# Banded attention and a two-layer product on one core: 200 transposes that nobody reads, two products moved behind the last first product, and a new order of every step

## The chip, the core and the metric

The kernel runs on one core of one Trainium2 chip. The metric is device time in microseconds (us). Three runs of the kernel before gave 1057.28, 1058.74 and 1061.05 us; the median is 1058.74.

## What is computed

The input has 8 batches of 8 heads, 512 local and 32 global positions each, 64 numbers per head. Local queries see local keys within 32 positions and all global keys; global queries see everything. The attention's output, 4352 rows of 512, then goes through a product with `w_in`, an exact GELU and a product with `w_out`. All is float32. Cut to what matters:

```
k_all, v_all = concat([k_g, k_l]), concat([v_g, v_l])
out_g = softmax(q_g @ k_all.T / 8) @ v_all
s_ll  = where(|i - j| <= 32, q_l @ k_l.T / 8, -1e9)
out_l = softmax(concat([q_l @ k_g.T / 8, s_ll])) @ v_all
x     = concat([out_g, out_l]) as rows of 512 (8 heads x 64)
y     = gelu(x @ w_in) @ w_out          # 512 -> 2048 -> 512
```

## The kernel before, in words

**Units and chunks.** The attention of one batch, one half (256 queries) and one pair of heads is a unit; there are 64, and they are numbered here u0, u1, ... in the order of the loop over `units`. Four units fill one chunk of 256 rows, which then goes through the two products. There are 16 such chunks, and a 17th, key `"g"`, of the 256 global rows.

**Steps of one unit.** `kp` and `qp` (L361 to L369): transposes on TensorE that turn keys and queries, copied out of PSUM to `kt` and `qt` (for the first eight units, `NPE`; later ones are transposed by VectorE, DVE). `s` (L439): scores. L458 on DVE adds the mask and takes the maximum; L322 on ScalarE (ACT) takes the exponentials into `a_t`; `sg` (L592) are the scores of the global queries. L488 to L492 on DVE scale by the sum, and L499 and L504, on DVE or GpSimd (POOL), make the edge pieces `ge`. `t` (L513 to L516): transposes of the probabilities, copied to `ao`. `o` (L562 for the first eight units, L549 later): probabilities times values, copied to `xs`.

**Steps of one chunk.** `xh` and `xl` split a row in a coarse part and a remainder, so that three fast products (L726 to L728) make up a float32 one. The first product, `h`, runs over 16 blocks f of 128 columns, each of four pieces over the input; `ml_g` takes the GELU of two blocks at once into `gf`, which is split in `gh` and `gl`; the second product (L757 to L759) adds two blocks' worth into the accumulators `acc0` and `acc1`. `ml_e` copies them to `ob`, and `ml_w` sends `ob` out.

**Weights.** `w_in` and `w_out` come in 32 pieces (`wl`, `wraw`); five steps (`w_1` to `w_5`: two on ACT, one shift on DVE, a cast and a subtraction) split each in two parts, kept in `wi` and `wo`. Of the first `WB` pieces, those with index 1, 2, 4 or 5 in each seven go through the pool `wb` (4 buffers), all others through `wa` (3 buffers). The space of `wb` is later used by `gf`, `gh`, `gl`, `xh` and `xl`.

**What sets the order.** Each step is a node with an engine or a choice of engines, a due time, needs, and buffers that it takes and frees. A list scheduler at the end of the function simulates the engines with the durations in `DUR` and, among the steps that can start first, takes the one due first; the due times are shifted per kind by the tables `OFF` (all) and `OFF0` (first chunk). Every engine then runs its steps in that order: an instruction that waits holds up all behind it on its engine.

PSUM is split in pools of two banks: `ps_s`, `ps_t`, `ps_h`, and `ps_o` with `acc0` and `acc1`. The first four blocks of the first chunk's `h` also use these two accumulators, so that the step `("hc", (0,0), 0, 0)` takes the buffer `acc`.

Of the kernel before, what the change touches and what calls it, by code (L numbers as in the profile page):

```python
# [8 lines left out]
F32 = mybir.dt.float32  # L9
# [4 lines left out]
AF = mybir.ActivationFunctionType  # L14
# [44 lines left out]

PORT = {"w3", "w4", "w5", "k2", "q1", "k1", "q2", "tgl", "b", "n", "nf", "ns", "vc", "vl", "gvc", "gvl", "xh", "xl", "gh", "gl", "gn"}  # L60

EARLY = {"gh": "a", "gl": "p", "gvc": "va", "gvl": "p", "k1": "a", "nf": "pv", "ns": "pv", "q1": "va", "vc": "va", "vl": "v", "xh": "va", "xl": "vp"}
LATER = {"gh": "va", "gl": "p", "gvc": "a", "gvl": "p", "k1": "va", "nf": "v", "ns": "pv", "q1": "va", "vc": "va", "vl": "p", "w4": "va", "w5": "pv", "xh": "a", "xl": "vp"}

OFF = {
    "ah": 3.7, "al": 7.1, "b": -0.8, "c": -23.8, "e": -38.8, "g": -16.9, "gagh": 2.4, "gagl": -24.7,
    "gah": -46.1, "gal": 17.6, "gex": 34.4, "gh": 11.4, "gl": 15.6, "glv": -3.1, "gmin": -0.7,
    "gn": 10.2, "go": -12.2, "gsh": 11.8, "gsl": -92.2, "gt": -6.0, "gvc": -51.6, "gvl": 28.8,
# [3 lines left out]
    "sga": -22.9, "sgc": -11.8, "t": 0.3, "tg": -5.3, "tgh": -13.8, "tgl": -30.7, "tk": 50.0,  # L72
    "tq": 106.4, "vc": -12.9, "vl": -42.1, "vm": -35.6, "w1": 67.7, "w2": -35.9, "w3": 0.2,
    "w4": 1.4, "w5": -5.6, "wl": 4.2, "x": 20.7, "xh": -24.9, "xl": -12.1,
}
OFF0 = {
    "ah": 6.2, "al": 2.7, "b": -8.0, "c": -4.3, "e": 8.2, "g": -11.9, "gagh": -12.8, "gagl": -27.4,
    "gah": 23.2, "gal": -25.7, "gex": 19.5, "gh": 2.9, "gl": 2.2, "glv": -5.1, "gmin": -5.1,
    "gn": -23.1, "go": 34.0, "gsh": -28.1, "gsl": -33.9, "gt": 7.9, "gvc": 55.3, "gvl": -10.2,
# [12 lines left out]
HQ = 4  # L92
NPE = 8
UNP = 100
WB = 14


@with_exitstack
def attn_mlp(ctx, tc, q_l, k_l, v_l, q_g, k_g, v_g, w_in, w_out, out):
    nc = tc.nc  # L100
    B, H, S, D = q_l.shape
    SG = q_g.shape[2]
    DM = H * D
# [10 lines left out]
    ap_ = ctx.enter_context(tc.tile_pool(name="ap", bufs=1))  # L114
# [557 lines left out]
    def gu_o(e, g, i):  # L672
        a = [late["agt"][:, n] for n in range(4)] + [late["agg"][:, i]]
        o = ps_s.tile([P, 2, 2, D], F32, name="go", tag="s")
        st[g, "o"] = o
        for n in range(5):
            nc.tensor.matmul(out=o, lhsT=a[n].rearrange("p h l q -> p (h l q)"),  # L677
                             rhs=late["vgs"][:, 2 * n:2 * n + 2], start=(n == 0), stop=(n == 4))

    def gu_sh(e, g, i):  # L680
        o = st[g, "o"]
        t = ap_.tile([P, 2, D], F32, name="gos", tag="gos")
        st[g, "os"] = t
        nc.scalar.activation(out=t, in_=o[:, :, 1, :], func=AF.Copy)

    def gu_sl(e, g, i):
        t = st[g, "os"]
        nc.vector.tensor_add(out=t, in0=st[g, "o"][:, :, 0, :], in1=t)

    def gu_x(e, g, i):  # L690
        t = ps_s.tile([P, 2, 2, SG], F32, name="gx", tag="s")
        st[g, "x"] = t
        nc.tensor.transpose(out=t, in_=st[g, "os"], identity=ident)

    def gu_yh(e, g, i):
        st[g, "c"] = c = ap_.tile([P, SG], F32, name="gc", tag="gc")
        for j in range(2):
            pr = slice(64 * j, 64 * j + 64)
            nc.scalar.activation(out=c[pr], in_=st[g, "x"][pr, j, 1, :], func=AF.Copy)

    def gu_yl(e, g, i):
        b, p = g[0], 2 * g[1] + i
        for j in range(2):
            pr = slice(64 * j, 64 * j + 64)
            nc.vector.tensor_add(out=late["xg"][pr, p, b * SG:b * SG + SG], in0=st[g, "x"][pr, j, 0, :], in1=st[g, "c"][pr])


    def ml_xh(e, key, p):
# [108 lines left out]
    for n, u in enumerate(units):  # L817
# [25 lines left out]
        else:  # L843
# [52 lines left out]
        if g and odd:  # L896
# [9 lines left out]
            for i in range(2):  # L906
# [11 lines left out]
                step(("gyh", g, i), gu_yh, (g, i), "a", g0 + 7.0 + 2 * i, [("gx", g, i)], [("gc", (g, i))])  # L918
                step(("gyl", g, i), gu_yl, (g, i), "v", g0 + 7.3 + 2 * i, [("gyh", g, i)], [], [("s", (g, i, "x")), ("gc", (g, i))])

    LAG = LAGS
    for n, key in enumerate(keys):
        C0, W = C * n, C / NF
# [209 lines left out]
```

## Time and profile before

| What | us |
|---|---|
| median of three runs | 1058.74 |
| the profiled execution's own time | 1058.35 |
| its span, first to last instruction | 1056.5 |
| TensorE busy | 1023.0 (97%) |
| ACT, DVE, POOL busy | 745.4, 716.1, 355.4 |

The profile is of one execution. PE is TensorE, SPq the queue from which SyncE issues DMAs. Lines are those of the kernel before. In a timeline a row gives the start, the duration from the first start to the last end of the instructions merged in it, engine, line, operation, output and inputs, and in brackets the idle time of the engine ahead of it with what ended it. Matmuls are pipelined: the time that one costs is the distance from its start to the next start, not its duration. In a table of stretches a row gives the stretch, its length, and for each engine the busy time with the number of instructions; then the granted clock of TensorE as a share of full speed, the DMA share and GB/s.

### The profile page before, as it was taken

To read this page: it belongs to the slowest core of one execution; us is meant where nothing else is said; L and a number is where in the kernel's file an instruction comes from. 1 tells how busy PE (TensorE), PEld (TensorE's weight loads), DVE (VectorE), ACT (ScalarE), POOL (GpSimd) and SP (SyncE) were. 2 spreads that over 40 slices of the span, in tenths; PEclk is the share of its full clock that TensorE was granted. 3 is DMA by queue.
4 is the path that set the end of the run, shared out by engine and by line. 5 is a ranking of instruction groups with operands and counts; after the bars stand their busy time and mean duration, and the time that the engine had idled before them with its cause. 6 is when DMAs were issued, how large, how long until landed. Compare 5 with 4: busy or idle time off the path is not lost.

```text
span 1056.5 us, 21637 instructions
## 1 busy us (share of the span) xinstructions
PE 1023.0 (97%) x7096; PEld 912.2 (86%) x7096; DVE 716.1 (68%) x2168; ACT 745.4 (71%) x1650; POOL 355.4 (34%) x407
## 2 busy tenths in 40 slices
PE   4799999999999999999999999999999999999997
PEld 3488789889899989998899988999899988999896
DVE  5898866775768767777868777677877778670000
ACT  5886887677769686787679677777778677873221
POOL 3232345334333434234323523233223433243120
PEclk9899999999999999999999999999999999999999
DMA  8656333322222332223222232223222332110000
GB/s 242 204 146 196 86 83 64 77 51 68 46 60 37 64 68 49 55 52 78 49 61 38 63 71 46 51 53 77 51 62 38 65 69 48 41 25 21 1 21 21
DMA packets 273233, 71.27 MB, mean 67 GB/s; under 512 B 258528, under 2 KB 266720, under 8 KB 273120
## 3 DMA queue, kind: packets, MB, share of 16 engines
q1 hardware_dynamic: 269808, 65.03, 27.5%
q10 hardware_dynamic: 3312, 4.85, 1.5%
q8 instruction: 56, 0.92, 0.4%
q14 instruction: 57, 0.47, 0.1%
HBM read 60.88 MB, written 8.91 MB: 66 GB/s over the span
## 4 chain that ended last, share of the span: by engine, by line
PE 88%; DMA 4%; ACT 3%; DVE 2%; SPq 1%; issue 1%; POOL 0%; ACTq 0%; DVEq 0%; POOLq 0%
PE h L726 12%; PE h L728 11%; PE h L727 11%; PE acc L757 11%; PE acc L758 11%; PE acc L759 11%; PE o L549 5%; PE s L439 5%; PE t L513 3%; PE go L677 2%; PE sg L592 2%; PE t L514 1%; DMA wraw<-in_moe_w_out_dram 1%; DMA wraw<-in_moe_w_in_dram 1%; ACT a_t L322 1%; DMA vr<-in_v_l_dram 1%
## 5 line engine op out<-in xcount | busy, mean ns | idle before, releaser
L163 POOL TENSOR_TENSOR gl<-gf,gh 128x512 fp32r<-128x512 f32 x135 | 177.2, 1312 | 461.7 <-DVE gh L158 259.9
L726 PE MATMUL h<-xh,wi 128*128 128x256 f32 x1088 | 314.9, 289 | 1.3 <-ACT xh L156 1.3
L727 PE MATMUL h<-xl,wi 128*128 128x256 f32 x1088 | 303.8, 279 | 0.7 <-POOL xl L163 0.4
L728 PE MATMUL h<-xh,wi 128*128 128x256 f32 x1088 | 303.6, 279 | 0.0
L757 PE MATMUL acc<-wo,gh 128*128 128x512 f32 x544 | 220.4, 405 | 1.4 <-ACT gh L156 1.4
L758 PE MATMUL acc<-wo,gl 128*128 128x512 f32 x544 | 215.5, 396 | 0.3 <-DVE gl L163 0.3
L759 PE MATMUL acc<-wo,gh 128*128 128x512 f32 x544 | 215.6, 396 | 0.0
L726 PEld LDWEIGHTS h<-xh,wi 128*128 128x128 f32 x1088 | 204.2, 188 | 12.5 <-ACT xh L156 1.7
L727 PEld LDWEIGHTS h<-xl,wi 128*128 128x128 f32 x1088 | 204.7, 188 | 7.2 <-DVE xl L163 0.6
L728 PEld LDWEIGHTS h<-xh,wi 128*128 128x128 f32 x1088 | 204.2, 188 | 0.0
L322 ACT ACT_TABLE_LOAD x129 | 165.5, 1283 | 40.3 <-PE h L728 38.6
L322 ACT ACTIVATE gf<-h 128x512 f32<-128x512 f32 x136 | 81.3, 598 | 78.8 <-PE h L728 76.2
L759 PEld LDWEIGHTS acc<-wo,gh 128*128 128x128 f32 x544 | 102.5, 188 | 24.6
L322 ACT ACTIVATE a_t<-a_t,sm 128x192 f32<-128x192 f32 (+1 forms) x256 | 117.0, 459 | 1.2 <-DVE sm L464 0.5
L757 PEld LDWEIGHTS acc<-wo,gh 128*128 128x128 f32 x544 | 102.5, 188 | 15.1 <-ACT gh L156 1.6
L758 PEld LDWEIGHTS acc<-wo,gl 128*128 128x128 f32 x544 | 102.7, 189 | 13.8 <-DVE gl L163 0.6
L163 POOL TENSOR_TENSOR vs<-vr,vs 128x512 fp32r<-128x512 f32 x56 | 72.7, 1298 | 120.0 <-ACT vs L156 56.3
L458 DVE CUSTOM_DVE_ANT_0 a_t<-s,mask 128x192 f32<-128x192 f32 (+1 forms) x256 | 80.8, 369 | 27.8 <-PE s L439 27.6
L533 DVE TENSOR_TENSOR at<-t,at 128x512 fp32r<-128x512 f32 x112 | 67.8, 619 | 23.6 <-ACT at L156 22.0
L156 ACT ACTIVATE at<-t 128x512 fp32r<-128x512 f32 x112 | 59.2, 542 | 23.9 <-PE t L516 10.4
L549 PE MATMUL o<-at,vs 128*128 128x256 f32 x448 | 74.3, 288 | 0.3 <-DVE sm L464 0.2
L549 PEld LDWEIGHTS o<-at,vs 128*128 128x128 f32 x448 | 63.0, 188 | 8.4 <-issue 2.1
(121 smaller groups left out, 1618.5 us busy)
## 6 DMA issues: line engine op xcount, KB each, us to landing
raws<-in_v_l_dram SPq DMA_DIRECT2D x64, 128.0 KB, 2.4
out_dram<-ob SPq DMA_DIRECT2D x32, 256.0 KB, 2.1
raws<-in_k_l_dram SPq DMA_DIRECT2D x224, 36.0 KB, 1.9
vr<-in_v_l_dram SPq DMA_DIRECT2D x116, 64.0 KB, 2.1
raws<-in_q_l_dram SPq DMA_DIRECT2D x224, 32.0 KB, 1.9
wraw<-in_moe_w_out_dram SPq DMA_DIRECT2D x12, 512.0 KB, 4.0
wraw<-in_moe_w_in_dram SPq DMA_DIRECT2D x11, 512.0 KB, 4.6
wraw<-in_moe_w_in_dram ACTq DMA_DIRECT2D x5, 512.0 KB, 4.4
```

Source lines behind the costliest of these rows:

```text
L156: nc.scalar.activation(out=out, in_=in_, func=AF.Copy)
L163: (nc.vector if e == "v" else nc.gpsimd).tensor_sub(**kw)
L322: nc.scalar.activation(func=func, **kw)
L458: nc.vector.tensor_tensor_reduce(out=a_t[:, j, aoff[half][i]:aoff[half][i] + w], in0=s[:, c:c + w], in1=masks[half][:, c:c + w], scale=1.0 ...
L533: nc.vector.tensor_sub(out=at[:, 1], in0=st.pop((u, "t", j))[:, :n * P].rearrange("p (n q) -> p n q", q=P), in1=at.bitcast(F32)[:, 0])
L549: nc.tensor.matmul(out=o[:, :, qsl], lhsT=l.rearrange("p s e -> p (s e)"), rhs=r, start=(n == 0), stop=(n == 3), skip_group_check=True)
L726: nc.tensor.matmul(out=h, lhsT=hi, rhs=xh, start=(c == 0 and not (key == (0, 0) and f < HQ and f % 2)), stop=False, skip_group_check=True)
L727: nc.tensor.matmul(out=h, lhsT=hi, rhs=xl, start=False, stop=False, skip_group_check=True)
L728: nc.tensor.matmul(out=h, lhsT=lo, rhs=xh, start=False, stop=(c == NCC - 1), skip_group_check=True)
L757: nc.tensor.matmul(out=acc[t], lhsT=gh[:, f % 2, tsl], rhs=hi, start=(f == 0), stop=False)
L758: nc.tensor.matmul(out=acc[t], lhsT=gl[:, f % 2, tsl], rhs=hi, start=False, stop=False)
L759: nc.tensor.matmul(out=acc[t], lhsT=gh[:, f % 2, tsl], rhs=lo, start=False, stop=(f == NF - 1))
```

## The change

A new step `dm` runs two 128x128 transposes of the identity into the bank `acc1`; nothing reads them. There are 100 such steps in a chain, due last of all, so that the scheduler puts one wherever TensorE would be idle by its own times. The first takes the buffer `acc` and the hundredth frees it, and the first chunk's first product takes the same buffer: it comes behind all 200 transposes. The first of them needs the first keys' transposes.

```
+    def st_dm(e, i):
+        if i == 0:
+            st["dm"] = ps_o.tile([P, DM], F32, name="dm", tag="acc1")
+        for n in range(2):
+            nc.tensor.transpose(out=st["dm"][:, n * P:n * P + P], in_=ident, identity=ident)
...
+NDM = 100
+NF32 = 8
...
+    for i in range(NDM):
+        step(("dm", i), st_dm, (i,), "t", 1e4, [("dm", i - 1) if i else ("tk", units[0])], [("acc", "dm")] if not i else [], [("acc", "dm")] if i == NDM - 1 else [])
```

In the chunk `"g"` the second products of blocks 12 to 15 now need the last piece of the last first product. Those of 14 and 15 needed it already, through the GELU; 12 and 13 are the two that move.

```
             step(("mo", key, f), ml_o, (key, f), "t", C0 + W * (f + LAG) + 1.0,
-                 [("gl", key, f // 2), ("mo", key, f - 1) if f else None, ("mo", keys[n - 1], NF - 1) if n and not f else None] + ([("w5", 2 * f + 1)] if not n else []),
+                 ([("hc", key, NF - 1, NCC - 1)] if key == "g" and f >= NF - 4 else []) + [("gl", key, f // 2), ("mo", key, f - 1) if f else None, ("mo", keys[n - 1], NF - 1) if n and not f else None] + ([("w5", 2 * f + 1)] if not n else []),
```

`WB` falls from 14 to 10, so that two weight pieces more go through the pool of three buffers. The planner's own durations and engines change in a few entries, and most of the shifts in `OFF` and `OFF0`; one line of many:

```
-    "tk": 0.65, "tkn": 0.75, "tqn": 0.45, "tq": 0.44, ...
+    "tk": 0.65, "tkn": 0.6, "tqn": 0.33, "dm": 0.22, "tq": 0.44, ...
...
-WB = 14
+WB = 10
...
-    "ah": 3.7, "al": 7.1, "b": -0.8, "c": -23.8, "e": -38.8, "g": -16.9, "gagh": 2.4, "gagl": -24.7,
+    "ah": 3.7, "al": 7.1, "b": -0.8, "c": -21.0, "dm": 16.9, "e": -33.2, "g": -16.9, "gagh": 8.1,
```

`NF32` names the units whose scores use unsplit keys and queries; it is 8 as `NPE` is, so nothing follows from it. The results of the global queries' step are kept per unit (`st[g, i, "o"]` for `st[g, "o"]`), so that two may be under way at once.

Because the due times move, the order of every engine is new. Three places follow. The first is TensorE around the start of the first product `h`. Before, it stands behind the scores of the sixth unit:

```order
L562 MATMUL o_597<-ao_593,vr 64x128
L562 MATMUL o_597<-ao_589,vr 64x128 x2
L439 MATMUL s<-kt,qt 128x192 x2
L439 MATMUL s<-kt,qt 128x224 x2
L369 MATMUL qp<-ident,raws 128x128 x2
L726 MATMUL h<-xh,wi 128x256
L727 MATMUL h<-xl,wi 128x256
L728 MATMUL h<-xh,wi 128x256
```

Ahead of it lie 7 `kp`, 7 `qp`, 6 `s`, 5 `sg`, 4 `t` and 4 `o`. In the changed kernel the same place reads:

```order
L572 MATMUL o_921<-ao_906,vr 64x128 x2
L332 MATMUL dm<-ident 128x128 x22
L602 MATMUL sg<-kt,gs 128x256
L332 MATMUL dm<-ident 128x128 x2
L523 MATMUL t<-ident,a_t_147 128x128 x2
L524 MATMUL t<-ident,ge 128x128
L526 MATMUL t<-ident,ge 128x128
L332 MATMUL dm<-ident 128x128 x2
L523 MATMUL t<-ident,a_t_147 128x128 x2
L524 MATMUL t<-ident,ge 128x128
L736 MATMUL h<-xh,wi 128x256
L737 MATMUL h<-xl,wi 128x256
```

Ahead of it now lie 8 `kp`, 8 `qp`, 7 `s`, 7 `sg`, 6 `t`, 5 `o` and the 200 transposes `dm`; the last `t` is that of u5. Behind it the first chunk's two products alternate without much between them.

The second place is ACT around the exponentials of the eighth unit, u7, which write `a_t_147`. Before, they follow the seventh GELU:

```order
L322 ACTIVATE gf<-h 128x512
L199 ACTIVATE wraw<-wraw 128x512
L203 ACTIVATE wraw<-wraw 128x512
L322 ACT_TABLE_LOAD
L322 ACTIVATE a_t_147,sm<-a_t_147,sm 128x192
L322 ACTIVATE a_t_147,sm<-a_t_147,sm 128x224
```

Now they follow the second:

```order
L324 ACTIVATE gf<-h 128x512
L205 ACTIVATE wraw<-wraw 128x512
L158 ACTIVATE gh<-gf 128x512
L188 DMA wraw<-in_moe_w_out_dram 128x1024
L201 ACTIVATE wraw<-wraw 128x512
L205 ACTIVATE wraw<-wraw 128x512
L324 ACT_TABLE_LOAD
L324 ACTIVATE a_t_147,sm<-a_t_147,sm 128x192
L324 ACTIVATE a_t_147,sm<-a_t_147,sm 128x224
```

Five GELUs and the weight steps between them have moved behind u7's exponentials.

The third place is the end of TensorE's program. The numbers of `gh` tell which blocks a second product uses. Before (`gh_13795` is of blocks 12 and 13, `gh_13837` of 14 and 15):

```order
L757 MATMUL acc0_13580<-wo_140,gh_13795 128x512
L758 MATMUL acc0_13580<-wo_140,gl_13797 128x512
L759 MATMUL acc0_13580<-wo_140,gh_13795 128x512
L757 MATMUL acc1_13581<-wo_140,gh_13795 128x512
L758 MATMUL acc1_13581<-wo_140,gl_13797 128x512
L759 MATMUL acc1_13581<-wo_140,gh_13795 128x512
L726 MATMUL h_13782<-xh_13479,wi_139 128x256
L727 MATMUL h_13782<-xl_13480,wi_139 128x256
L728 MATMUL h_13782<-xh_13479,wi_139 128x256
L757 MATMUL acc0_13580<-wo_140,gh_13837 128x512
L758 MATMUL acc0_13580<-wo_140,gl_13839 128x512
L759 MATMUL acc0_13580<-wo_140,gh_13837 128x512
```

And now (`gh_13996` is of blocks 12 and 13):

```order
L736 MATMUL h_13983<-xh_13680,wi_139 128x256
L737 MATMUL h_13983<-xl_13681,wi_139 128x256
L738 MATMUL h_13983<-xh_13680,wi_139 128x256
L767 MATMUL acc0_13781<-wo_140,gh_13996 128x512
L768 MATMUL acc0_13781<-wo_140,gl_13998 128x512
L769 MATMUL acc0_13781<-wo_140,gh_13996 128x512
L767 MATMUL acc1_13782<-wo_140,gh_13996 128x512
L768 MATMUL acc1_13782<-wo_140,gl_13998 128x512
L769 MATMUL acc1_13782<-wo_140,gh_13996 128x512
L767 MATMUL acc0_13781<-wo_140,gh_13996 128x512
L768 MATMUL acc0_13781<-wo_140,gl_13998 128x512
L769 MATMUL acc0_13781<-wo_140,gh_13996 128x512
```

Twelve matmuls, those of blocks 12 and 13, moved from between the last pieces of `h` to behind the last of them; the twelve of blocks 14 and 15 stay at the very end.

## Rows read from the trace of the kernel before

**Rows 1.** Busy time by stretch: stretch, length, busy per engine (instructions), clock, DMA.
```profile
56.70:200.00 143.30, 137.25 (x949) 121.20 (x949) 112.73 (x321) 111.73 (x246) 51.10 (x58) 0.99 0.46 113
189.00:200.00 11.00, 9.28 (x71) 8.46 (x70) 8.48 (x23) 8.07 (x18) 2.99 (x6) 1.00 0.42 94
200.00:1040.00 840.00, 839.92 (x5929) 758.73 (x5928) 561.44 (x1731) 588.52 (x1296) 288.26 (x312) 1.00 0.24 51
1045.00:1056.50 11.50, 5.05 (x15) 3.07 (x13) 0.69 (x1) 2.42 (x4) 0.00 (x0) 0.80 0.18 46
```
**Rows 2.** Timeline of TensorE, three stretches from 56 to 75: start, duration, instruction.
```profile
56.71 0.36 PE L726 MATMUL h<-xh,wi 128*128 128x256 f32 x1
...
64.36 0.38 PE L369 MATMUL qp<-ident,raws 128*128 128x128 f32 x2
64.58 0.38 PE L513 MATMUL t<-ident,a_t 128*128 128x128 f32 x2
...
65.44 0.97 PE L439 MATMUL s<-kt,qt 64*128 64x192 f32 x8
66.73 1.96 PE L562 MATMUL o<-ao,vr 128*64 128x128 f32 x16 [0.33 <-ACT ao L156]
...
74.36 0.59 PE L592 MATMUL sg<-kt,gs 128*128 128x256 f32 x2
74.60 0.58 PE L757 MATMUL acc<-wo,gh 128*128 128x512 f32 x1
```
**Rows 3.** Busy time by stretch, columns as in rows 1: up to the last `xl`.
```profile
15.30:58.30 43.00, 32.43 (x177) 23.65 (x177) 38.12 (x110) 37.62 (x96) 10.27 (x12) 0.88 0.72 210
```
**Rows 4.** Timeline of VectorE near 57 us.
```profile
56.70 1.63 DVE L163 TENSOR_TENSOR xl<-xs,xh 128x256 fp32r<-128x256 f32 x3
```
**Rows 5.** Timeline of GpSimd near 108 us: the edge pieces of one unit.
```profile
108.20 1.03 POOL L499 TENSOR_TENSOR ge<-a_t,sm 128x256 f32<-128x256 f32 x1 [9.52 <-DVE sm L489]
109.19 0.40 POOL L504 TENSOR_TENSOR ge<-a_t,sm 128x128 f32<-128x128 f32 x1
```
**Rows 6.** Timeline of TensorE, 20 to 25 us.
```profile
20.76 2.00 PE L439 MATMUL s<-kt,qt 64*128 64x192 f32 x8
22.69 0.69 PE L513 MATMUL t<-ident,a_t 128*128 128x128 f32 x2
23.17 0.42 PE L514 MATMUL t<-ident,ge 128*128 128x128 f32 x1
23.38 0.42 PE L516 MATMUL t<-ident,ge 128*128 128x128 f32 x1
```
**Rows 7.** The chain of waits near 100 us: start, length, what held the chain.
```profile
99.50 3.59 DMA wraw<-in_moe_w_out_dram
...
104.40 1.28 ACT L322
```
**Rows 8.** Timeline of TensorE at 110 us: `o` of the seventh unit.
```profile
110.01 3.46 PE L562 MATMUL o<-ao,vr 128*64 128x128 f32 x16 [2.33 <-ACT ao L156]
```
**Rows 9.** Timeline of all engines, the end of the program.
```profile
1044.97 0.28 PE L728 MATMUL h<-xh,wi 128*128 128x256 f32 x1
...
1046.65 0.50 PE L757 MATMUL acc<-wo,gh 128*128 128x512 f32 x1 [1.41 <-ACT gh L156]
...
1047.78 0.39 PE L759 MATMUL acc<-wo,gh 128*128 128x512 f32 x1
1048.01 0.40 PE L757 MATMUL acc<-wo,gh 128*128 128x512 f32 x1
...
1049.40 0.63 PE L758 MATMUL acc<-wo,gl 128*128 128x512 f32 x1
...
1049.84 3.34 SPq L772 DMA_DIRECT2D out_dram<-ob  x6
...
1051.77 0.60 ACT L156 ACTIVATE ob<-acc 128x512 f32<-128x512 f32 x1 [1.96 <-PE acc L759]
1052.40 0.85 ACTq L772 DMA_DIRECT2D out_dram<-ob  x2
```

More of the change, by code (lines that the diff above doesn't have):

```diff
@@ L60 @@
 PORT = {"w3", "w4", "w5", "k2", "q1", "k1", "q2", "tgl", "b", "n", "nf", "ns", "vc", "vl", "gvc", "gvl", "xh", "xl", "gh", "gl", "gn"}
-EARLY = {"gh": "a", "gl": "p", "gvc": "va", "gvl": "p", "k1": "a", "nf": "pv", "ns": "pv", "q1": "va", "vc": "va", "vl": "v", "xh": "va", "xl": "vp"}
+EARLY = {"gh": "a", "gl": "p", "gvc": "va", "gvl": "p", "k1": "a", "nf": "pv", "ns": "pv", "q1": "va", "vc": "a", "vl": "p", "xh": "va", "xl": "vp"}
 LATER = {"gh": "va", "gl": "p", "gvc": "a", "gvl": "p", "k1": "va", "nf": "v", "ns": "pv", "q1": "va", "vc": "va", "vl": "p", "w4": "va", "w5": "pv", "xh": "a", "xl": "vp"}
 OFF = {
-    "ah": 3.7, "al": 7.1, "b": -0.8, "c": -23.8, "e": -38.8, "g": -16.9, "gagh": 2.4, "gagl": -24.7,
-    "gah": -46.1, "gal": 17.6, "gex": 34.4, "gh": 11.4, "gl": 15.6, "glv": -3.1, "gmin": -0.7,
-    "gn": 10.2, "go": -12.2, "gsh": 11.8, "gsl": -92.2, "gt": -6.0, "gvc": -51.6, "gvl": 28.8,
[3 rows of a table removed]
-    "sga": -22.9, "sgc": -11.8, "t": 0.3, "tg": -5.3, "tgh": -13.8, "tgl": -30.7, "tk": 50.0,
-    "tq": 106.4, "vc": -12.9, "vl": -42.1, "vm": -35.6, "w1": 67.7, "w2": -35.9, "w3": 0.2,
-    "w4": 1.4, "w5": -5.6, "wl": 4.2, "x": 20.7, "xh": -24.9, "xl": -12.1,
+    "ah": 3.7, "al": 7.1, "b": -0.8, "c": -21.0, "dm": 16.9, "e": -33.2, "g": -16.9, "gagh": 8.1,
+    "gagl": -19.5, "gah": -47.7, "gal": 17.6, "gex": 39.3, "gh": 6.1, "gl": 21.5, "glv": -10.5,
+    "gmin": -3.2, "gn": 19.3, "go": -13.5, "gsh": 12.2, "gsl": -93.4, "gt": -3.0, "gvc": -53.7,
[3 rows of a table added]
+    "sga": -51.5, "sgc": -11.8, "t": 0.5, "tg": -6.2, "tgh": -21.3, "tgl": -31.9, "tk": 56.9,
+    "tq": 106.4, "vc": -16.8, "vl": -42.0, "vm": -57.4, "w1": 62.7, "w2": -35.8, "w3": 0.2,
+    "w4": 1.4, "w5": -1.9, "wl": 4.2, "x": 22.4, "xh": -24.9, "xl": -9.8,
 }
 OFF0 = {
-    "ah": 6.2, "al": 2.7, "b": -8.0, "c": -4.3, "e": 8.2, "g": -11.9, "gagh": -12.8, "gagl": -27.4,
-    "gah": 23.2, "gal": -25.7, "gex": 19.5, "gh": 2.9, "gl": 2.2, "glv": -5.1, "gmin": -5.1,
-    "gn": -23.1, "go": 34.0, "gsh": -28.1, "gsl": -33.9, "gt": 7.9, "gvc": 55.3, "gvl": -10.2,
[6 rows of a table removed]
-}
+    "ah": 7.7, "al": 41.8, "b": -8.0, "c": -2.3, "dm": -7.8, "e": 8.2, "g": -12.0, "gagh": 6.8,
+    "gagl": -27.4, "gah": 27.8, "gal": -29.5, "gex": 17.8, "gh": 1.9, "gl": 1.7, "glv": -5.0,
+    "gmin": -5.0, "gn": -24.1, "go": 34.0, "gsh": -28.3, "gsl": -35.1, "gt": 7.9, "gvc": 55.3,
[6 rows of a table added]
+}
+NDM = 100
+NF32 = 8
 WLE = "as"
@@ L674, in gu_o @@
         o = ps_s.tile([P, 2, 2, D], F32, name="go", tag="s")
-        st[g, "o"] = o
+        st[g, i, "o"] = o
         for n in range(5):
@@ L680, in gu_sh @@
     def gu_sh(e, g, i):
-        o = st[g, "o"]
+        o = st[g, i, "o"]
         t = ap_.tile([P, 2, D], F32, name="gos", tag="gos")
-        st[g, "os"] = t
+        st[g, i, "os"] = t
         nc.scalar.activation(out=t, in_=o[:, :, 1, :], func=AF.Copy)
     def gu_sl(e, g, i):
-        t = st[g, "os"]
-        nc.vector.tensor_add(out=t, in0=st[g, "o"][:, :, 0, :], in1=t)
+        t = st[g, i, "os"]
+        nc.vector.tensor_add(out=t, in0=st[g, i, "o"][:, :, 0, :], in1=t)
     def gu_x(e, g, i):
         t = ps_s.tile([P, 2, 2, SG], F32, name="gx", tag="s")
-        st[g, "x"] = t
-        nc.tensor.transpose(out=t, in_=st[g, "os"], identity=ident)
+        st[g, i, "x"] = t
+        nc.tensor.transpose(out=t, in_=st[g, i, "os"], identity=ident)
     def gu_yh(e, g, i):
-        st[g, "c"] = c = ap_.tile([P, SG], F32, name="gc", tag="gc")
+        st[g, i, "c"] = c = ap_.tile([P, SG], F32, name="gc", tag="gc")
         for j in range(2):
             pr = slice(64 * j, 64 * j + 64)
-            nc.scalar.activation(out=c[pr], in_=st[g, "x"][pr, j, 1, :], func=AF.Copy)
+            nc.scalar.activation(out=c[pr], in_=st[g, i, "x"][pr, j, 1, :], func=AF.Copy)
     def gu_yl(e, g, i):
@@ L704, in gu_yl @@
             pr = slice(64 * j, 64 * j + 64)
-            nc.vector.tensor_add(out=late["xg"][pr, p, b * SG:b * SG + SG], in0=st[g, "x"][pr, j, 0, :], in1=st[g, "c"][pr])
+            nc.vector.tensor_add(out=late["xg"][pr, p, b * SG:b * SG + SG], in0=st[g, i, "x"][pr, j, 0, :], in1=st[g, i, "c"][pr])
     def ml_xh(e, key, p):
@@ L849, in attn_mlp @@
             kb, qb = [("kt", u)], [("qt", u)]
-        w = n < NPE
+        w = n < NF32
         step(("k1", u), st_k0 if w else st_k1, (u,), "av", s0 - 4.0, [("tk", u)], [("kt" if w else "k1", u)], kb if w else [], early=n < 8, port=n >= NPE)
```

20 rows, old and new, of tables (DUR, OFF, OFF0) are left out of this document.

## Prediction

> **What bounds the kernel now.** I read the busy time by stretch first. From 200 to 1040 us TensorE is busy 839.92 of 840 us [rows 1]: the reader is to see that nothing is to be gained there, and that the time is TensorE's work plus what it loses at both ends. The second stretch, 56.7 to 200, has 143.3 - 137.25 = 6.05 us of idle time; the last, from 1045 on, has 11.5 - 5.05 = 6.45, at a granted clock of 0.80. For the start I go to the timeline of TensorE. The first product begins at 56.71 [rows 2]; all before is attention, for which TensorE mostly waits. What it waits for is seen in the stretch from 15.3 to 58.3: VectorE (DVE) is busy 38.12 of 43 us [rows 3], and the last `xl` of DVE, which the first product needs, ends at 56.70 + 1.63 = 58.3 [rows 4]. So DVE's queue sets the start, and only 4.9 us of its time there are idle. The end is read from the timeline of all engines [rows 9].
>
> **Prices on TensorE.** From starts in the fast stretch [rows 2]: two transposes of `qp` 64.58 - 64.36 = 0.22, so 0.11 each and 0.33 for the three of `kp`; `t` 65.44 - 64.58 = 0.86; `s` 0.97; `o` 1.96; `sg` 74.60 - 74.36 = 0.24. One second-product matmul costs 1048.01 - 1047.78 = 0.23, one first-product matmul about half, 0.12 [rows 9]. In the slow stretch one transpose costs 23.38 - 23.17 = 0.21, `s` 2.00 [rows 6]; these are the two levels 2.4 and 1.2 GHz.
>
> **The end: the two held products.** Now the last `h` matmul starts at 1044.97 and its slot ends at 1045.09. GELU, split and `gh` then take until 1046.65, an idle 1.41 us; later matmuls have durations of 0.63 for 0.40 [rows 9], the clock having fallen after that idle time; the last accumulator is copied at 1051.77. In the new order the twelve matmuls of blocks 12 and 13 stand in this wait. They take 12 x 0.23 = 2.8 us, so the last `h` ends 2.8 earlier, at 1042.3; its `gh` is there 1.6 later (1046.65 - 1045.09), at 1043.9, and the moved matmuls cover until 1045.1. The twelve that remain need 2.8 more at the fast price, if the clock stays, and it has no idle time to fall after. The copy of `acc1` starts some 0.2 later, at 1048.1 instead of 1051.77: 3.65 us. The last DMAs behind it also have to wait for SyncE's queue: six issues that take 3.34 us from the first, now 1049.84 [rows 9]. The first half's copy ends 2.5 us earlier (`acc0` is done six matmuls ahead of `acc1`), so the queue could be free only 2.5 earlier at worst. Between 2.5 and 3.65 I take 3.2, since four of the six issues are out before the second copy and the 3.34 holds a wait for it. If the clock fell all the same, seven matmuls at 0.43 for 0.23 would take back 1.4. **-3.2 us.**
>
> **The start: ahead of the first product.** The scheduler may not begin `h` before the hundredth `dm`; so more attention stands ahead of it. Before: 7 x 0.33 + 7 x 0.22 + 6 x 0.97 + 5 x 0.24 + 4 x 0.86 + 4 x 1.96 = 22.15 us of useful work at the fast price, so 56.7 - 22.15 = 34.55 are lost. Now: 8 x 0.33 + 8 x 0.22 + 7 x 0.97 + 7 x 0.24 + 6 x 0.86 + 5 x 1.96 = 27.83.
>
> When does `h` begin? Just ahead of it is `t` of u5, which needs DVE's scaling of u5 and POOL's `ge`. On DVE the last `xl` comes after 118 instructions, 117 before: as much work, with two weight shifts and two weight subtractions fewer. With the same waits it ends at 58.3, with none of the 4.9 us of idle time at 53.4. I take 54, near the lower end: the mix is lighter, and the waits of that stretch were on TensorE's slow `s` and on ACT, whose copies and exponentials stand earlier now. Behind `xl` stand 33 more DVE instructions up to the scaling of u5; at 38.12 / 110 = 0.347 each [rows 3] they take 11.4. Then `ge`, 109.19 + 0.40 - 108.20 = 1.4 [rows 5], and `t`, 0.9. `h` begins at 54 + 13.7 = 67.7 (67.1 to 72.0), and 67.7 - 27.8 = 39.9 are lost, 5.3 more than before (4.7 to 9.6).
>
> The 200 dummies fit in that: 27.8 + 200 x 0.11 = 49.8 of TensorE's time by 67.7, if they run fast; they cost nothing as long as DVE is behind. The gain that they bring by the clock is within the 4.9 above: the first units' `s` and `t` end up to half as late, but DVE has little to wait for.
>
> **The start: behind the first product.** Between 56.7 and 200 TensorE loses the 6.05 of idle time, and `o` at 110 takes 3.46 for 1.96, as the clock falls after a wait of 2.33 [rows 8]: 7.5 in all. That wait is ACT's: u6's `ao` stands behind weight steps that wait for a load (3.59 from issue to landing), a table load of 1.28 and u7's exponentials [rows 7]. In the new order u7's exponentials stand behind the second GELU, when their TensorE work is far ahead; and as the first product starts 11 us later, weights have 11 us more of lead. The first chunk's products then run almost unbroken, 2.8 us a block, and attention for the second chunk lies ready. I let go all of it but the 11 - 9.28 = 1.7 at 189 to 200 [rows 1], where the next chunk's `xh` and `xl` follow an `o` closely, which the new order has as well. **+5.3 - 5.8 = -0.5 us.** The bounds: nothing stays (-1.7 more), or other stalls as long come in their place (+5.8).
>
> **The rest.** `WB` = 10 sends two weight pieces more through three buffers, and on SyncE's queue the loads of keys and values of u2 to u7 now stand ahead of two weight loads that they followed. I cost it at nothing: the later `h` covers it; without the cover ACT waits for a landing, 3.6 us [rows 7]. The table shifts move steps all through the program, but where DVE and ACT have 560 and 590 us of work in 840 [rows 1] a moved step delays nobody; from nothing to +2 if an order has gaps there, and I take nothing, as the stretch shows none. `NF32` and the kept names do nothing.
>
> **Sum.** -3.2 - 0.5 = -3.7 from the profiled execution's own 1058.35 (span 1056.5 and 1.85 around it), which stands 0.4 below the median of 1058.74: **1054.7 us**.
>
> **Rivals.**
>
> *The dummies get in the way (slower).* Place: TensorE ahead of `h`. If they don't lift the clock they cost 0.21 each, 42 us, and every real step that is ready waits behind those placed ahead of it: TensorE then needs 27.8 + 42 = 69.8 us, and with its own work slow too, up to 2 x 27.8 + 42 = 97.6. It decides as soon as TensorE's own sum passes the 67.7 of DVE's path. At the 80 between these ends `h` begins 12.3 later: 1067. For it: through the first 24 us the transposes and `s` ran slowly although TensorE worked in stretches. Against it: just then it ran `s` and then transposes without a pause from 20.76 on [rows 6], and soon after `o` and all others cost the fast price; so a stretch that is part transposes did not keep the clock down.
>
> The Trainium skill, "TensorE: Matmul & The Clock Gate", section "Part 4: PE-mode transpose", speaks against this change: it says that the full clock doesn't engage for transposes, since they don't count as busy time the way products do. By it this rival would hold. The rows above lean the other way, but no run here yet shows transposes alone.
>
> *The start gives back what it saves (no change).* The work put off comes due together: chunk 0's products without attention between, then `o` of u6 and u7 and the splits of chunk 1 close to one another. If stalls of 5.8 come back there, 1060.5; at half, 1057.6. For it: DVE has 38 of 43 us of work at the start, and no order makes that less. Against it: from 60 us on its work isn't what ends the span.
>
> *The start wins more.* DVE runs without a wait (`h` at 67.1), no stall is left behind it, and the end gives the full 3.65: 1054.7 - 0.6 - 1.7 - 0.45 = 1052.0.
>
> *Late on both.* DVE waits as before (`h` at 72.0) and the stalls stay: 1054.7 + 4.3 + 5.8 = 1064.8.
>
> **How the numbers follow.** 0.3%, 3.2 us, is about what a measurement of this kernel tells from no change: faster is below 1055.6, slower above 1061.9. The forecast has 0.41 (its own range 1053 to 1055.5), the larger gain 0.13, the start that gives back 0.29, the dummies in the way 0.12, late on both 0.05. So faster 0.54, the same 0.29, slower 0.17. The range of 8 in 10 leaves out most of the dummies' case and the far end of the larger gain: 1050.0 to 1062.5.
>
> **What would show it.** The end: no idle time of TensorE behind the last `h`, durations of 0.40 to the last matmul, the copy of `acc1` 1048.1 - 1042.2 = 5.9 us behind the last `h` (6.8 before), and the 1.96 of idle time ahead of it [rows 9] turned to 0.8 (6 x 0.23 less the 0.60 of a copy). The start: dummies 0.11 apart from about 15 us on; the last `xl` of the first chunk near 54, `h` near 68; no wait for `ao` above 1 us behind it, and less than 2 us of idle time between `h` and 200. I am wrong if the dummies start 0.21 apart past 25 us; if real steps start late behind dummies with their inputs long ready; or if idle time of 5 us and more shows up between 68 and 200, or at all after 200.

## The result: 0.2% slower, with the end as forecast and the start not

The changed kernel takes 1062.08 us (median of 22 runs, 1060.20 to 1064.26), the kernel before 1060.12 (22 runs, 1057.28 to 1063.21). The ratio is 1.0020, 95% interval 1.0011 to 1.0029: some 2 us slower, where 4 us faster was forecast. The profiled execution took 1061.96 us, its span is 1060.2; that is 0.1 below the median of its kernel, while the profiled execution of the kernel before, 1058.35, stands 1.8 below its median. So the two profiles differ by 3.6 us where the medians differ by 2.0. From the page: TensorE busy 1037.8 us (98%), ACT 741.7, DVE 717.4, POOL 361.1; TensorE has 14.8 us more, the 200 transposes being among it.

The same stretches as [rows 1, 3], of the changed kernel: stretch, length, busy time of TensorE, its weight loads, DVE, ACT and POOL with instructions, then granted clock, DMA share, GB/s.

```profile
15.30:58.30 43.00, 38.41 (x279) 31.34 (x278) 37.55 (x115) 33.71 (x90) 9.92 (x11) 0.96 0.66 187
56.70:200.00 143.30, 137.88 (x964) 123.52 (x965) 108.23 (x305) 103.62 (x226) 47.94 (x53) 0.98 0.45 114
...
78.60:200.00 121.40, 121.40 (x846) 109.23 (x845) 91.50 (x257) 94.30 (x203) 42.62 (x46) 0.99 0.42 103
...
200.00:1040.00 840.00, 839.90 (x5941) 759.90 (x5940) 567.91 (x1753) 594.43 (x1311) 295.58 (x318) 1.00 0.24 52
1045.00:1060.20 15.20, 10.01 (x50) 8.03 (x48) 0.69 (x1) 2.42 (x4) 0.94 (x1) 0.92 0.13 35
```

From 200 to 1040 TensorE is as busy as before, 839.90 for 839.92. Behind 78.6 it has no idle time at all up to 200. So nearly all that was lost at the start lies ahead of 78.6, where the first product now begins. TensorE's timeline there, to be read beside [rows 2]:

```profile
59.68 3.88 PE L332 MATMUL dm<-ident 128*128 128x128 f32 x34
...
69.24 2.62 PE L332 MATMUL dm<-ident 128*128 128x128 f32 x22
75.39 1.22 PE L602 MATMUL sg<-kt,gs 128*128 128x256 f32 x2 [3.53 <-DVE sm L468]
...
78.61 0.56 PE L736 MATMUL h<-xh,wi 128*128 128x256 f32 x1
```

The first `h` stands at 78.61, not at 67.7. Ahead of it `sg` of u6 waits 3.53 us for DVE, and after that wait two of its matmuls take 1.22 us for 0.59, and `h` 0.56 for 0.36: the level of 1.2 GHz. The end, to be read beside [rows 9]:

```profile
1049.13 0.28 PE L738 MATMUL h<-xh,wi 128*128 128x256 f32 x1
1049.25 0.40 PE L767 MATMUL acc<-wo,gh 128*128 128x512 f32 x1
...
1054.27 2.68 SPq L782 DMA_DIRECT2D out_dram<-ob  x6
...
1054.62 0.40 PE L769 MATMUL acc<-wo,gh 128*128 128x512 f32 x1
1055.05 0.60 ACT L158 ACTIVATE ob<-acc 128x512 f32<-128x512 f32 x1 [0.80 <-PE acc L769]
```

The second products follow the last `h` without a gap, durations stay at 0.40 to the last, the copy of `acc1` starts 5.92 us behind the last `h`, and ACT idles 0.80 ahead of it.

For the comparisons below I add up one figure from TensorE's records: the time that it loses. Each matmul is worth the median distance to the next start that its form has in the kernel before; the dummies are worth nothing; what is left of a stretch is lost. It is a count from one execution of each kernel, and executions differ: two of the hold alone (a kernel of the next section), of 1054.09 and 1059.67 us, differ by 5.1 us in the time lost to 200. So a difference of a few us in this count is read here together with the medians.

| kernel | first `h` | lost ahead of it | lost from `h` to 200 | lost to 200 |
|---|---|---|---|---|
| before | 56.7 | 35.9 | 12.8 | 48.7 |
| changed | 78.6 | 52.7 | 2.4 | 55.1 |

So the start costs 6.4 us more, the end gives some 3.3 back (1060.2 - 1049.13 = 11.07 behind the start of the last `h`, 11.53 before, and 2.8 of moved work in it), and the sum, 3.1, is near the 3.7 by which the spans differ. The medians say the same of the start: 2.0 slower in all, with an end that the experiments put at 3.6 to 4.0, makes 5.6 to 6.0.

**Where the start lost it.** Two queues, before and changed. SyncE's queue around 40 us, first of the kernel before (the load at 39.60 is weight piece 14, the next one keys of u6 and u7):

```profile
39.60 0.77 SPq L182 DMA_DIRECT2D wraw<-in_moe_w_in_dram  x1
42.77 0.93 SPq L345 DMA_DIRECT2D raws<-in_k_l_dram  x2
```

and of the changed one:

```profile
39.56 0.93 SPq L355 DMA_DIRECT2D raws<-in_k_l_dram  x2
...
42.08 1.31 SPq L358 DMA_DIRECT2D raws<-in_k_l_dram  x2
43.49 0.53 SPq L184 DMA_DIRECT2D wraw<-in_moe_w_in_dram  x1
```

The keys went ahead of the weight piece, and its load is issued 3.9 us later. In the changed order ACT's steps on this piece stand ahead of u4's exponentials. ACT's timeline:

```profile
47.73 0.67 ACT L201 ACTIVATE wraw<-wraw 128x512 int32<-128x512 uint16 x1 [4.31 <-DMA wraw<-in_moe_w_in_dram]
...
49.25 0.44 ACT L324 ACTIVATE a_t<-a_t,sm 128x192 f32<-128x192 f32 x1
```

ACT stands still for 4.31 us with u4's attention behind it. And DVE, from the last `xl` to u6's mask:

```profile
55.29 2.19 DVE L165 TENSOR_TENSOR xl<-xs,xh 128x256 fp32r<-128x256 f32 x3
...
59.79 0.42 DVE L615 TENSOR_TENSOR sgr<-sg,sgr 64x256 f32<-64x256 f32 x1 [1.14 <-ACT sgr L608]
...
69.56 0.69 DVE L209 SCALAR_TENSOR_TENSOR wraw<-wraw 128x512 int32<-128x512 int32 x1 [2.08 <-ACT wraw L205]
...
71.77 0.69 DVE L502 TENSOR_TENSOR a_t<-a_t,sm 128x512 f32<-128x512 f32 x1
72.38 1.10 DVE L209 SCALAR_TENSOR_TENSOR wraw<-wraw 128x512 int32<-128x512 int32 x1
...
74.67 0.35 DVE L468 CUSTOM_DVE_ANT_0 a_t<-s,mask 128x192 f32<-128x192 f32 x1
```

DVE too waits for a weight piece, and works on two of them (from 69.56 and from 72.38) around u5's scaling and ahead of u6's mask, on which `sg` of u6 waits.

### The profile page after: what moved, and what is told of

It is laid out like the page before. It is cut to its first block, busy times and chain, and to the rows that moved or that the text cites. A ratio compares the mean times of both kernels' runs of the same rounds, so it can differ in the third digit from the quotient of the medians.

```text
span 1060.2 us, 22053 instructions
## 1 busy us (share of the span) xinstructions
PE 1037.8 (98%) x7296; PEld 933.2 (88%) x7296; DVE 717.4 (68%) x2175; ACT 741.7 (70%) x1644; POOL 361.1 (34%) x408
## 4 chain that ended last, share of the span: by engine, by line
PE 94%; DMA 3%; DVE 1%; ACT 1%; issue 0%; SPq 0%; ACTq 0%; DVEq 0%
PE h L736 13%; PE h L738 12%; PE acc L767 12%; PE h L737 12%; PE acc L769 12%; PE acc L768 12%; PE o L559 6%; PE s L449 5%; PE t L523 3%; PE go L687 2%; PE sg L602 2%; PE t L524 1%; DMA wraw<-in_moe_w_out_dram 1%; PE o L572 1%; DMA wraw<-in_moe_w_in_dram 1%; PE gt L647 1%
```

## Experiments

Theory: late weight loads, and weight steps that stand ahead of attention, put the first `h` off; the dummies cost nothing. Rivals: the dummies hold the real work up; the gate in front of `h` costs the time; the end is worth less than it seems. Several kernels were timed together with the kernel before; each such group is called a comparison, and each ratio is to the runs of the kernel before in the same one. The ratio is not exactly that of the two medians. Where two kernels stand in different comparisons, the difference of their times is less certain than that of their ratios.

**The parts: the hold, the dummies, WB.** The hold alone, and the changed kernel without it:

```
-  ([("hc", key, NF - 1, NCC - 1)] if key == "g" and f >= NF - 4 else []) + [("gl", ...
+  [("gl", ...
```

> The kernel before with one edit alone: the second products of blocks 12 and 13 of the last chunk wait for the last first product. All other engines keep their order. Theory (the hold is worth what the trace of the change shows at its end, where the lost time of TensorE behind the last first product is gone): 3.2 to 3.5 us less than before, ratio 0.997, the span near 1053. Rival (the end gains only in company of the new tables): ratio 0.999 to 1.001.

> The changed kernel without the hold; dummies, WB = 10 and the new tables stay. If the parts simply add up: 3.2 to 3.5 us more than the changed kernel, near 1065.5, ratio to before 1.005. If the hold is worth less here: ratio 1.002 to 1.003.

Measured: the hold alone 1056.74, ratio 0.9963 (0.9949 to 0.9978), 3.6 us less; once more, in another comparison, 1056.58 and 0.9967 (0.9951 to 0.9982). Without it the changed kernel takes 1065.25, 1.0042 (1.0026 to 1.0059). Alone, the hold is worth what was forecast, and its rival is out. In the changed kernel it is worth 3.2 us by the medians (1065.25 and 1062.08, of two comparisons) and 2.3 by the ratios (1.0042 and 1.0020), so that it may be worth a little less there.

The dummies taken out, the order kept:

```
-        for n in range(2):
+        for n in range(2 if i == 0 else 0):
```

> The changed kernel with the same order of all engines, but 198 of the 200 dummy transposes are not issued: the steps stand in the order and are empty, so the first h stays behind the same attention. Theory (DVE's queue, held by weights, sets the first h; the dummies lie in TensorE's waits): h at 77 to 81, since without them the clock falls more often in the waits; time from 1061 to 1065, ratio to before 1.001 to 1.005. Rival (the dummies themselves hold the real steps up): h 5 us and more earlier, near 72, ratio 0.993 to 0.997.

Measured: 1062.60, 1.0022 (1.0010 to 1.0033), `h` at 78.45: no change. So the dummies neither hold `h` up nor help here. Yet they do lift the clock. Of the changed kernel, dummies and then u0's scores; up to these scores TensorE has run only transposes:

```profile
8.88 2.82 PE L332 MATMUL dm<-ident 128*128 128x128 f32 x12
...
12.34 1.90 PE L332 MATMUL dm<-ident 128*128 128x128 f32 x12
...
14.39 1.03 PE L449 MATMUL s<-kt,qt 64*128 64x192 f32 x8
```

and the same scores without dummies:

```profile
13.39 1.86 PE L449 MATMUL s<-kt,qt 64*128 64x192 f32 x8
```

The scores run at 2.4 GHz behind the dummies and at 1.2 without. TensorE is faster, and then waits for the same DVE and ACT.

`WB = 12` for 10, with the same tables:

> The changed kernel with WB = 12 for 10: one weight piece more goes through the pool of four buffers, and the scheduler orders anew with the same tables; 100 dm steps and the hold stay. Theory (the waits of ACT and DVE for weight pieces at 43 to 48 and 63 to 68 us put the first h off): at least one of the two waits is gone, h at 70 to 75, time 1055 to 1059. Rival (the longer queue of attention ahead of h and not the weights): h at 77 to 80, time within 1.5 us of the changed kernel's.

Measured: `h` at 71.36, as the theory had it, but 1081.68 and 1.0205 (1.0180 to 1.0229). Up to 100 us TensorE had lost 7 us less than in the changed kernel; then the new order shows waits up to 535 us (2.56 at 263, 1.99 at 344, 1.74 at 514), and behind 200 some 20 us more are lost than in the changed kernel. Up to 80 us ACT waits 9.0 us for weight loads instead of 15.0, and DVE no longer than 0.8 at a time for ACT's weight steps. That fits the theory, but everything else moved as well, so it does not show the cause, and the total says nothing on it: a number that a scheduler reads changes the whole order. From here on I keep the order and move single steps, by giving them another time behind the scheduler's sort:

```
     order.sort(key=lambda e: e[:2])
+    order = [(moved.get(x["name"], t), i, x) for t, i, x in order]
+    order.sort(key=lambda e: e[:2])
```

**Moving the suspects.** u4 to u7 are `(0,1,0)` to `(0,1,3)`; `n` is the scaling, `m` mask and maximum, `w1` to `w5` the steps of a weight piece.

```
act:   w1, w2 of piece 14 behind u4's exponentials; w3 behind the last xl, w4, w5 behind it
dve:   n of u5, m of u6 ahead of w3 to w5 of pieces 13 and 18
both:  both moves;   bothempty: both, dummies not issued;   actempty: act, dummies not issued
```

> The changed kernel with one weight piece (index 14) moved in the order: its two ACT steps stand behind the exponentials of u4 for ahead of them, its DVE shift behind the last xl, its cast and subtraction behind these. All else keeps its place. Theory (ACT's wait of 4.31 us for this load holds up u4 and with it the splits): that wait is gone, the last xl ends near 54.5 for 57.5, h at 75 to 76 for 78.6, time 1058.5 to 1060, ratio to before 0.998 to 1.000. Rival (the wait is hidden, DVE has other work): xl and h within 1 us of the changed kernel's, 1062.

> The changed kernel with u5's scaling and u6's mask and maximum on DVE ahead of two weight pieces (13 and 18) for behind them, and all else in place. Theory (DVE, held by a late weight load at 67.5 to 69.6 and then by the two pieces, sets sg of u6 and t of u5, and so h): h at 72.5 to 74, no wait of TensorE above 1.5 us at 72 to 75, time 1056 to 1058, ratio 0.996 to 0.998. Rival (the wait only moves into chunk 0's first products, whose weight pieces are later now): h earlier, time within 1.5 us of 1062.

> Both moves together. Theory: they add up less what the 22 dummies ahead of sg take: h at 69 to 71, time 1053.5 to 1056, ratio 0.993 to 0.996. Rival (weights late for the first products give it back): h at 69 to 71, but 1058 and more.

> Both moves, and 198 of the 200 dummy transposes not issued. If dummies never stood in the way: the same as both moves with them, within 1 us, or later by a slower clock. If the dummies block once DVE is early: h 1 to 2 us earlier than with them.

> The changed kernel with the one weight piece moved behind u4's exponentials, and 198 of the 200 dummy transposes not issued. If the dummies are worth something once ACT's wait is gone (as the pair with both moves says: 3.6 us): h 1.5 to 3 us later than with them (72.7), time 1059.5 to 1061.5, ratio 0.999 to 1.001. If that pair was chance: within 1 us of 1057.6.

| kernel | us | ratio (95%) | first `h` | lost ahead | `h` to 200 | to 200 |
|---|---|---|---|---|---|---|
| act | 1057.62 | 0.9967 (0.9954 to 0.9980) | 72.7 | 46.8 | 1.9 | 48.7 |
| dve | 1061.63 | 1.0014 (1.0001 to 1.0027) | 73.4 | 47.5 | 6.2 | 53.8 |
| both | 1057.01 | 0.9964 (0.9947 to 0.9981) | 72.6 | 46.7 | 4.0 | 50.7 |
| bothempty | 1060.66 | 0.9996 (0.9984 to 1.0008) | 73.8 | 47.9 | 5.5 | 53.4 |
| actempty | 1060.55 | 1.0016 (1.0003 to 1.0029) | 75.5 | 49.6 | 3.3 | 52.9 |

One piece moved on ACT and DVE brings the first `h` 5.9 us forward and the time 4.5 down (5.6 by the ratios 1.0020 and 0.9967), more than expected. With it the start loses no more than that of the kernel before (48.7), and the medians agree: `act` is 3.0 us below the kernel before, where the hold alone gives 3.6 to 4.0. Its rows, the last `xl` and the first `h`:

```profile
51.83 2.20 DVE L165 TENSOR_TENSOR xl<-xs,xh 128x256 fp32r<-128x256 f32 x3
```

```profile
72.69 0.36 PE L736 MATMUL h<-xh,wi 128*128 128x256 f32 x1
```

The move on DVE also brings `h` forward, by 5.2 us, and gives nearly all of it back, as its rival said. DVE and TensorE behind it:

```profile
80.62 0.69 DVE L209 SCALAR_TENSOR_TENSOR wraw<-wraw 128x512 int32<-128x512 int32 x1 [5.55 <-ACT wraw L205]
```

```profile
82.29 3.25 PE L572 MATMUL o<-ao,vr 128*64 128x128 f32 x16 [3.32 <-DVE ao L160]
```

The next weight piece's load is no earlier: ACT waits 5.65 us for it, and DVE 5.55 for ACT's step, with u5's `ao` behind, and `o` runs slowly after a wait of 3.32. Both moves together add little to the first alone: that part of the theory (that they add up) fell.

With ACT's wait gone the dummies are worth something: 3.6 us between `both` and `bothempty`, of one comparison, where the slowest run with them is faster than the fastest without. Between `act` and `actempty`, of two comparisons, it is 2.9 us by the medians and 5.2 by the ratios (0.9967 and 1.0016). The stretch from 38 to 56 of `both` and of `bothempty`; the granted clock is 0.99 and 0.81:

```profile
38.00:56.00 18.00, 15.21 (x116) 12.32 (x114) 15.00 (x38) 12.92 (x36) 3.14 (x5) 0.99 0.52 136
```

```profile
38.00:56.00 18.00, 13.48 (x74) 10.15 (x73) 14.09 (x45) 13.90 (x37) 3.25 (x6) 0.81 0.57 147
```

**Why the load was late.** By its place on SyncE's queue, or for want of a buffer:

```
sp:    the loads of keys for u6, u7 behind that of weight piece 14; nothing else
```

> The changed kernel with one edit on SyncE's queue: the load of weight piece 14 stands ahead of the loads of keys for u6 and u7 (seven issues) for behind them; ACT, DVE, GpSimd and TensorE keep their order. Theory (its place in the queue makes the load late; its buffer is free near 40): issued at 39.5 to 40.5 for 43.49, ACT's wait of 4.31 falls to at most 1.3, the last xl at 54 to 55.5, h at 74 to 76, time 2.5 to 4 us below the changed kernel, ratio to before 0.998 to 1.000. Rival (it waits for a buffer of the pool of three): issued at 42.5 or later, h and time within 1 us of the changed kernel's.

Measured: 1058.49, 0.9983 (0.9968 to 0.9998), 3.6 us below the changed kernel; `h` at 74.29, 50.9 lost to 200. SyncE's queue, and ACT:

```profile
40.65 0.39 SPq L184 DMA_DIRECT2D wraw<-in_moe_w_in_dram  x1
```

```profile
44.53 0.68 ACT L201 ACTIVATE wraw<-wraw 128x512 int32<-128x512 uint16 x1 [0.76 <-DMA wraw<-in_moe_w_in_dram]
```

and the last `xl`:

```profile
53.83 2.21 DVE L165 TENSOR_TENSOR xl<-xs,xh 128x256 fp32r<-128x256 f32 x3
```

It was the queue: the load went out 2.8 us earlier and ACT's wait fell from 4.31 to 0.76. The buffer was free. The last `xl` ends at 56.04, 1.4 earlier than in the changed kernel and later than the 54 to 55.5 expected; moving the piece's own steps (`act`) brings it to 54.03.

**The gate.** In the kernel of `act`, the dummies behind 55.7 us of the planner's time taken out, and real products in their place:

```
fill1: 11 pieces of h, blocks 0 to 3, ahead of t of u4, 5 behind o of u4; blocks 4 to 7 ahead of o of u5
fill2: also GELU, gh, gl of chunk 0 one place earlier each; blocks 8 to 15 as early as their weights
```

> The changed kernel with the one weight piece moved, without the dummies placed behind 55.7 us of the planner's time; in their place the 16 pieces of the first four blocks of chunk 0's first product (11 ahead of t of u4, 5 behind o of u4), and blocks 4 to 7 ahead of o of u5. Theory (the dummies keep real work out of waits that they fill): h near 57.5 for 72.7; TensorE has 5.7 us less to do behind 72, time 1052 to 1055, ratio 0.992 to 0.995. Rival (GELU and the second products, whose places on ACT are as before, wait as long): new waits of TensorE of 3 us and more at 78 to 95, time 1056 to 1058.

> As the kernel before in this list, and the GELUs of chunk 0 and their splits one place earlier each on ACT and GpSimd (the first ahead of the load that ACT waits for at 70 to 74), blocks 8 to 15 of the first product earlier as far as their weights allow. Theory: the waits at 78 to 95 go, time 1050 to 1053, ratio 0.990 to 0.993. Rival (two more table loads and the weights' landings hold ACT): within 1.5 us of the other or slower.

Measured: 1059.55, 1.0004 (0.9990 to 1.0017), and 1072.01, 1.0130 (1.0112 to 1.0148): both theories fell. In `fill1` the waits that the rival named are there, and the time is worse than it said; of `fill2` the rival ("or slower") holds. Two rows of the first:

```profile
57.59 0.36 PE L736 MATMUL h<-xh,wi 128*128 128x256 f32 x1
...
80.31 0.58 PE L736 MATMUL h<-xh,wi 128*128 128x256 f32 x1 [4.78 <-ACT kt L158]
```

`h` starts 15.1 us earlier than in `act`, and the kernel is slower (1.0004 for 0.9967): TensorE then waits 4.78 at 75 and 2.57 at 94, where ACT's steps stand as before (53.3 lost to 200). In the second it waits 3.91 and 5.01 for weights at 110 and 120. So a late `h` is not a loss by itself: with `h` at 57.6 this start loses 4.6 us more than that of `act`, in waits for ACT.

**The dummies in the start of before.** The hold, and 30 `dm` steps with the tables and `WB = 14` of the kernel before; all orders but for the 60 transposes are those of the hold alone:

> The kernel before with the hold and with 30 dm steps (60 transposes), its own tables and WB = 14: the order of all engines is that of the hold alone, with the 60 transposes in the waits of TensorE before 27 us. Theory (the start is set by DVE, ACT and loads, the clock of TensorE there costs nothing): h within 1 us of 56.3, time within 1.5 us of the hold alone (1056.7), ratio 0.995 to 0.998. Rival (the slow s and t at 14 to 25 us are on the path, and the transposes lift the clock there): h 2 to 4 us earlier, time 1053 to 1055, ratio 0.993 to 0.995.

> The kernel before with the hold alone, once more beside the next: ratio 0.9955 to 0.997.

> The hold and 60 transposes in TensorE's waits before 27 us, once more. If the clock is worth nothing there: within 1 us of the hold alone. If it is worth the 2 us that the profiled execution showed: 1.5 to 2.5 us below it, the intervals barely apart.

> The hold, the 60 transposes, and on ACT near 100 us u7's exponentials ahead of a weight piece that waits for its load, and u6's two copies to ao right behind them. Theory (o of u6 waits 3.1 us for these copies and then runs at the slow clock): o of u6 starts 2 to 3 us earlier, its wait is at most 1 us and the clock stays, 2.5 to 4.5 us below the kernel without the move: 1048 to 1051, ratio 0.990 to 0.9935. Rival (the delayed weight piece holds the second product of block 12): within 1 us of it.

Measured: 1052.95 and 0.9954 (0.9938 to 0.9971) in one comparison; in the other, beside the hold alone at 1056.58, 1053.98 and 0.9936 (0.9913 to 0.9958). That is 2.6 us below the hold, with intervals that just overlap; the slowest of its 6 runs took 1054.96, the fastest of 12 with the hold alone 1054.51. So the theory that the clock is worth nothing there fell. `o` of u0 in the hold alone, then with the 60 transposes:

```profile
25.27 1.94 PE L562 MATMUL o<-ao,vr 128*64 128x128 f32 x15
```

```profile
23.29 1.96 PE L570 MATMUL o<-ao,vr 128*64 128x128 f32 x16
```

In these two executions 2.0 us are won by 25 us. The other pair, of the first comparison, has this `o` at 24.59 and 24.11 and shows 0.5, and the hold's row above is from one of its slowest executions. What all of them share is the speed: u1's scores take 2.0 and 1.76 us in the two executions without the transposes, 1.03 and 1.02 with them. So TensorE's slow steps at the start are on the path, for 0.5 to 2.0 us by 25 us; where the rest of the 2.6 comes from is not shown. No other version here is faster: 6.2 and 6.6 us below the kernel before by the medians, 4.9 and 6.8 by the ratios. The last edit, u7's exponentials and u6's copies ahead of a weight piece, took the wait of `o` of u6 away:

```profile
107.50 2.12 PE L570 MATMUL o<-ao,vr 128*64 128x128 f32 x16 [0.36 <-ACT ao L157]
```

The same place without the edit:

```profile
107.87 3.36 PE L570 MATMUL o<-ao,vr 128*64 128x128 f32 x16 [3.12 <-ACT ao L157]
```

Yet 1054.12 and 0.9936 (0.9912 to 0.9960) are no gain. This execution was 2.3 us late from the first `h` on (56.74 for 54.41), ahead of all that was moved; counted from `h`, `o` starts 2.7 us earlier. What that wins comes back as waits that the execution without the edit does not have, 0.57 and 0.44 just behind, then 1.23 and, at 134, 2.04, which end with GpSimd, ACT and DVE. Two of them:

```profile
111.02 0.50 PE L766 MATMUL acc<-wo,gl 128*128 128x512 f32 x1 [0.57 <-POOL gl L164]
...
122.12 0.39 PE L735 MATMUL h<-xl,wi 128*128 128x256 f32 x1 [1.23 <-DVE xl L164]
```

## Why the prediction was wrong

- **The end, -3.2: right.** 3.3 by the rows, 3.6 and 4.0 by the hold alone, 2.3 to 3.2 in the changed kernel. The 5.9 us from the last `h` to the copy of `acc1`, the idle time of 0.8 and the durations of 0.40 are all as said.
- **The step that failed: "I cost it at nothing: the later `h` covers it".** That was said of the weight load that keys now stand ahead of on SyncE's queue. The cover does not exist, since the load is not waited for by `h` but by ACT, which has u4's exponentials behind it, and `h` itself comes later with u4. What the forecast set beside it, that without the cover ACT waits for a landing, 3.6 us, is what happened (4.31). Undoing the place on the queue alone gives 3.6 us back, moving the piece's steps 4.5, and with the latter the start is as good as that of the kernel before, where the forecast had it 0.5 better and the changed kernel lost 6.4.
- **`h` at 67.7: 10.9 too early.** Three parts. The last `xl` at 57.5 for 54: 3.5, ACT's wait. From there to the end of u5's scaling 15.0 (72.46 - 57.48) for 11.4: 3.6, of which 2.08 and 1.14 are waits of DVE for ACT. From the scaling to `h` 6.15 for 2.3: 3.9; here the forecast took `t` of u5 as the last thing ahead of `h`, when the order shows `sg` of u6 in front of it, whose buffer waits for u6's mask on DVE behind another weight piece, and which then runs at the slow clock.
- **"I take 54, near the lower end": wrong end.** That sum left DVE 0.6 us of idle time in the stretch up to 58.3; it is busy 37.55 of 43 us there, 38.12 before. The new order took old waits away and brought its own; without ACT's wait (`act`) the last `xl` does end at 54.
- **Behind the first product, -5.8: right in kind, too small.** 10.4 by the table, as the wait for `ao`, the slow stretch behind it and the smaller gaps all went. It offsets more than half of the +16.8 ahead of `h`: the two are one thing, since what TensorE does not do ahead of `h` lies ready behind it. `fill1` shows the trade from the other side.
- **The rival of the dummies in the way: out.** They run at 0.11 each from about 13 us on, but for the four behind the wait of 3.53, and taking them out changes nothing. The Trainium skill, "TensorE: Matmul & The Clock Gate", section "Part 4: PE-mode transpose", by which they would not count as work for the clock, does not agree with this trace: 34 of them in a row take 3.88 us at 59.68, 0.11 each, and the scores behind the first 24 run twice as fast as without. The forecast's own place for them (a gain "within the 4.9", little) is right for the changed kernel; in other starts they are worth more, 3.6 us in `both`, where ACT's wait is gone, and 2.6 in the start of the kernel before.
- **The base: 1.8 too low.** The sum starts from the profiled execution's 1058.35, and the median of 22 runs is 1060.12. Of the 7.4 us between forecast and result this is the choice of one execution; nearly all the rest is the start.
- **The range held the time, the sign did not.** A sum that starts at the median gives 1056.4, with the same wrong sign. The case that came is nearest to "late on both", with stalls ahead of `h` in the place of those behind it, and had 0.05.

What stays open: of the 10.9 us by which `h` came late, the load's place on the queue accounts for 4.3 (`sp`) and the piece's steps for 5.9 (`act`); for the rest it is not shown how much of DVE's 2.08 and of the tail of that chain is due to the smaller `WB`, and how much to the order; `wb12` brought `h` forward but changed everything else with it.

## What to carry to other kernels

When a new order moves a load behind others on a queue, look for the instruction that consumes it and for what stands behind that one on its engine; the price is that engine's wait, and here no later work of another engine covered it. The start time of the first big product is no measure of a start; count the time lost up to a fixed point, and in more than one execution, since here two of the same kernel differed by 5 us in it. Work that only keeps the clock up paid here where TensorE's own steps were on the path, and not where another engine's wait set it: so clear those waits first. And a wait that is taken away in one place shows its worth only in the total: in the last edit it came back elsewhere.

## What the runs showed of the hardware

Transposes alone bring the clock to the upper level and keep it there: the first 12 dummies take 2.82 us (0.22 from start to start), the 12 from 12.34 on 1.90, later ones 0.11 each. The clock fell after a wait of 2.70 (`o` took 3.71 for 1.96) and after the 3.53:

```profile
50.45 3.71 PE L572 MATMUL o<-ao,vr 128*64 128x128 f32 x16 [2.70 <-DVE ao L160]
```

It did not fall after a wait of 1.70 in `act` (0.70, then `t` at the fast price):

```profile
71.03 0.70 PE L602 MATMUL sg<-kt,gs 128*128 128x256 f32 x2 [1.70 <-DVE sm L468]
```

At the end of the kernel before [rows 9] it fell behind an idle time of 1.41 us and a further one of 0.28, 1.9 us after the first had ended: the durations go from 0.40 to 0.63 at 1048.55. So the length of one wait does not decide alone.
